# Two buffers and one sum of the last group, its reload's sequence, and the written unit order of a gated recurrent attention kernel

## The chip, the cores and the metric

The kernel runs on one core of one Trainium2 chip. A core has five engines that each work through a list of instructions in order: TensorE (PE, matrix multiplies), VectorE (DVE), ScalarE (ACT), GpSimd (POOL) and SyncE (SP, which here only issues DMAs). They wait for each other by semaphores. The metric is the time of one execution in microseconds of device time, the median of several.

## The reference

Two branches work on the same `x` (2048 rows of 512) and are mixed row by row by a gate.

```python
g = _sigmoid((x * gate_w).sum(-1, keepdims=True))
a = _A_ref(x, A_mem0, A_Wq, A_Wk, A_Wv, A_Wo, A_seg_len)
b = _B_ref(x, B_wq, B_wk, B_wv, B_wo, B_beta)
return g * a + (1 - g) * b
```

Branch A is a recurrence over 64 segments of 32 rows. Each segment takes the 8 memory rows that the segment before it left, puts its 32 rows behind them, and runs attention with 32 heads of 128 over these 40 rows:

```python
for s in range(n_seg):
    h = jnp.concatenate([mem, xs], axis=1)
    q, k, v = (jnp.einsum('btd,dhe->bhte', h, W) for W in (Wq, Wk, Wv))
    scores = jnp.where(mask[None, None], jnp.einsum('bhqe,bhke->bhqk', q, k) * scale, -1e9)
    o = jnp.einsum('bhqk,bhke->bhqe', _softmax(scores), v)
    o = jnp.einsum('bhte,hed->btd', o, Wo)
    mem = o[:, :M, :].copy()
    outs.append(o[:, M:, :])
```

So segment s+1 can't begin before segment s has its output's first 8 rows. Branch B is a linear-attention layer over 4 blocks of 512 rows with 32 heads of 16; it depends on nothing in branch A.

## The kernel before, in words

**The work.** Everything is built as a list of operations for each engine. A planner class (`Prog`) derives the waits from what each operation reads and writes; an operation that overwrites a buffer waits for the buffer's readers, DMAs included. The order on each engine is the order in which the operations are recorded, and from segment 0 on that is the order of the names in one long string, `A_ORDER`, of 4,509 units. Before it stand the loads, the projections of branch B and the gate (up to some 50.8 us in the profile).

**Names in the order.** `s.Kbx` and `s.Kby` are the two halves of the projection of keys for half b (16 heads) of segment s on PE (line 1272; 8 matmuls each), and so for Q and V; Q1 is split otherwise (line 1498). Small letters (`s.k0`, `s.v1`) are the evacuations from PSUM, `T..` the transposes on DVE, `Z` a bias matmul, `S` scores (lines 1558 and 1563), `X` the exponential, `Y` the mask (1576), `M` the row sums on PE (1591), `L` logarithm and exponential on ACT that make the reciprocal (1598, 1601), `N` and `n` the multiplications by it on DVE (1605) and POOL (1610). `s.PV` is the product with the values, called pv (1622) and pvL (1633) on PE; `E0` to `E3` evacuate it into `OT_sb`; `W0` to `W3` are the four output passes on PE, called wo (1359; 1371 in the last segment). `s.hm` turns the first 8 rows into the next segment's memory on DVE (1659 to 1664), `s.H` evacuates all rows to `WN` and `s.ws` stores them to DRAM (`aTd`). A `~` behind a name swaps ACT and DVE for that unit's evacuation.

**Left rows.** A segment has 40 rows, 8 more than a multiple of 32. The last 8 of each of the 4 segments of a group g are done together: `Lg.xl` gathers them (line 1297), `Lg.KL..`, `QL..` and `VL..` project them, and the values go to DRAM and back in another layout: a store when both halves are evacuated (line 1305) and the reload `Lg.VLt` (line 1313), which pvL of the group's segments reads. `Og.0` to `Og.3` are their output passes (ol on PE, line 1359), `Og.e` evacuates them to `WN` (olev), `Og.s` stores them to `aTl` (sto).

**The tail of a group.** `Tg.l` reloads 128 rows of both stores into `AR` (one DMA per segment and store, lines 1422 and 1424), `Tg.a` adds the two halves of `AR` on POOL (asum, 1428), `Tg.b` is branch B's output product on PE (brow, 1441; for the last group also browz, 1451), `Tg.t` scales it by 1 - g into AR's first half (t1, 1459; t1z, 1464), `Tg.f` multiplies, adds and stores the result (fin, 1471; out, 1473). Group 15 is the last; its fourth segment, 63, has its own short way: finz (1668) and four small stores (1672).

**Branch B.** `pj` and `pp` are late projections of the last block and their evacuations (lp on PE, line 830), `bS` scores (926), `bE` exponentials (947) and masks, `bP` the product with the values (979), `bT` what follows. `wl` loads one of eight pieces of Wo (line 540). The last bP is in segment 58; from there on the buffers `KTj` (keys) and `PT` (probabilities) of branch B are not used any more.

Of the kernel before, what the change touches and what calls it, by code (L numbers as in the profile page):

```python
# [1769 lines left out]
```

## Time and profile before

| what | us |
| --- | --- |
| median of 3 executions | 839.45 (837.83 to 843.68) |
| the profiled execution | 840.33 |
| its span, first to last instruction | 838.3 |
| PE busy in the span | 791.7 |
| DVE, ACT, POOL busy | 582.7, 566.0, 290.0 |
| mean granted clock of TensorE | 0.991 |

The profile is of one execution. "L1272" is line 1272 of the kernel before. "Busy" is the time in which an engine has an instruction under way; PE's matmuls are pipelined, so their ends overlap the next one's start. A bracket at the end of a timeline row holds the idle time of the engine before the row and what ended it. "SPq" rows are DMAs as SP issues them; they land later. The granted clock of TensorE is a share of its full speed.

### The profile page before, as it was taken

What the parts mean: (1) busy time and instruction counts of PE and PEld (TensorE: products, weight loads), DVE (VectorE), ACT (ScalarE), POOL (GpSimd) and SP (SyncE); (2) the same over time, 40 slices, a digit from 0 to 9 for tenths busy, and PEclk for the clock granted to TensorE, in tenths of its full rate; (3) what the DMA queues carried; (4) which work ended last, traced back from release to release, by engine and by line L of the source; (5) the groups of instructions that cost most, each with busy time, mean ns of one, the idle gap of its engine ahead of it and who ended that gap; (6) DMA issues with size and microseconds to landing.
All of it is one profiled execution on the core that took longest, in us unless ns stands there. A gap on an engine that the chain in (4) does not pass through costs nothing.

```text
span 838.3 us, 51677 instructions
## 1 busy us (share of the span) xinstructions
PE 791.7 (94%) x23285; PEld 487.1 (58%) x23291; DVE 582.7 (70%) x1469; ACT 566.0 (68%) x1368; POOL 290.0 (35%) x728
## 2 busy tenths in 40 slices
PE   8997999999999999999999999999999999999885
PEld 4544566555575656556556556566656556556553
DVE  4556677767677677787767686687676778687553
ACT  5544777877768667777657877685676775886452
POOL 4501443432424343342522434252233332453121
PEclk9998999999999999999999999999999999999998
DMA  8995332122222122112213031122122122121221
GB/s 330 415 373 180 88 93 73 39 65 71 52 63 81 38 63 62 46 45 78 64 30 94 28 78 46 42 51 70 54 71 72 35 57 66 39 52 41 74 79 52
DMA packets 100632, 72.34 MB, mean 86 GB/s; under 512 B 58068, under 2 KB 94524, under 8 KB 98876
## 3 DMA queue, kind: packets, MB, share of 16 engines
q1 hardware_dynamic: 99692, 68.24, 26.6%
q8 instruction: 182, 2.98, 1.5%
q10 hardware_dynamic: 720, 0.80, 0.3%
q14 instruction: 38, 0.31, 0.1%
HBM read 43.43 MB, written 25.58 MB: 82 GB/s over the span
## 4 chain that ended last, share of the span: by engine, by line
PE 74%; DVE 8%; ACT 7%; DMA 5%; issue 3%; POOL 2%; SPq 1%; ACTq 0%; DVEq 0%; POOLq 0%
PE ps L1272 35%; PE ps L1359 15%; PE ps L1498 6%; PE ps L1622 3%; PE ps L926 2%; PE ps L979 2%; DMA scr_kqd<-stgk 2%; ACT PT L947 2%; POOL PT L953 2%; PE ps L1558 1%; PE ps L692 1%; PE ps L1591 1%; PE ps L1441 1%; ACT R_sb L1601 1%; DVE oTt L1003 1%
## 5 line engine op out<-in xcount | busy, mean ns | idle before, releaser
L947 ACT ACTIVATE PT<-ps 128x512 bf16<-128x512 f32 x320 | 171.9, 603 | 55.2 <-PE ps L926 47.2
L953 POOL TENSOR_SCALAR_AFFINE_SELECT PT<-PT 128x128 bf16<-128x128 bf16 (+2 forms) x320 | 121.5, 380 | 213.5 <-ACT PT L947 195.1
L1272 PE MATMUL ps<-Wv_sb,xTp 128*32 128x512 bf16 x2048 | 144.0, 379 | 0.0
L1272 PE MATMUL ps<-Wk_sb,xTp 128*32 128x512 bf16 x2048 | 132.8, 379 | 1.8 <-DVE xTp L1664 1.5
L1359 PE MATMUL ps<-Wo_sb,OT_sb 128*32 128x256 bf16 x4032 | 125.2, 275 | 7.7 <-ACT OT_sb L377 3.6
L1359 PEld LDWEIGHTS ps<-Wo_sb,OT_sb 128*32 128x32 bf16 x4032 | 103.4, 97 | 29.5 <-ACT OT_sb L377 22.2
L1610 POOL TENSOR_TENSOR P_sb<-P_sb,R_sb 128x64 bf16<-128x64 bf16 x128 | 49.9, 390 | 160.9 <-ACT R_sb L1601 155.1
L377 ACT ACTIVATE OT_sb<-ps 128x320 bf16<-128x320 f32 x174 | 65.2, 439 | 36.5 <-PE ps L1633 35.8
L1272 PEld LDWEIGHTS ps<-Wk_sb,xTp 128*32 128x32 bf16 x2048 | 56.1, 97 | 52.1 <-DVE xTp L1664 7.8
L377 ACT ACTIVATE KN_sb<-ps 128x512 bf16<-128x512 f32 x98 | 58.8, 603 | 40.0 <-PE ps L1272 38.9
L377 ACT ACTIVATE QN_sb<-ps 128x256 bf16<-128x256 f32 (+1 forms) x148 | 64.6, 438 | 26.8 <-PE ps L1272 24.8
L1498 PE MATMUL ps<-Wq_sb,xTp 128*32 128x256 bf16 x2048 | 71.6, 273 | 2.4 <-DVE xTp L1664 2.0
L1284 DVE STREAM_TRANSPOSE QT_sb<-QN_sb 128x128 f32<-128x128 f32 (+1 forms) x192 | 63.2, 335 | 12.8 <-ACT QN_sb L377 10.5
L1272 PE MATMUL ps<-Wq_sb,xTp 128*32 128x512 bf16 x1024 | 70.2, 381 | 1.4 <-DVE xTp L1664 0.8
L1572 ACT ACTIVATE P_sb<-ps 128x224 bf16<-128x224 f32 x128 | 45.6, 358 | 34.1 <-PE ps L1563 28.6
L1284 DVE STREAM_TRANSPOSE KT_sb<-KN_sb 128x256 f32<-128x256 f32 x128 | 55.8, 437 | 18.4 <-ACT KN_sb L377 15.2
L379 DVE CAST V_sb<-ps 128x512 bf16<-128x512 f32 x80 | 54.8, 687 | 18.9 <-PE ps L1272 17.0
L1498 PEld LDWEIGHTS ps<-Wq_sb,xTp 128*32 128x32 bf16 x2048 | 54.6, 97 | 20.6 <-DVE xTp L1664 7.3
L1659 DVE STREAM_TRANSPOSE tt<-ps 128x256 f32<-128x256 f32 x63 | 28.3, 450 | 50.8 <-PE ps L1359 50.3
L379 DVE CAST OT_sb<-ps 128x320 bf16<-128x320 f32 x82 | 37.5, 486 | 28.6 <-PE ps L1633 27.7
L1605 DVE TENSOR_TENSOR P_sb<-P_sb,R_sb 128x160 bf16<-128x160 bf16 x128 | 42.3, 340 | 16.5 <-ACT R_sb L1601 15.7
L1272 PEld LDWEIGHTS ps<-Wv_sb,xTp 128*32 128x32 bf16 x2048 | 44.8, 95 | 12.9 <-ACT QN_sb L377 1.0
(143 smaller groups left out, 1413.7 us busy)
## 6 DMA issues: line engine op xcount, KB each, us to landing
scr_aTd<-WN SPq DMA_DIRECT2D x63, 128.0 KB, 2.1
AR<-scr_aTd SPq DMA_DIRECT2D x63, 96.0 KB
Wk_sb<-in_A_Wk_dram SPq DMA_DIRECT2D x4, 1024.0 KB, 11.1
Wq_sb<-in_A_Wq_dram SPq DMA_DIRECT2D x4, 1024.0 KB, 14.5
Wv_sb<-in_A_Wv_dram SPq DMA_DIRECT2D x4, 1024.0 KB, 13.8
Wo_sb<-in_A_Wo_dram SPq DMA_DIRECT2D x8, 512.0 KB, 7.4
scr_vld<-VNL SPq DMA_DIRECT2D x16, 256.0 KB, 2.1
VL<-scr_vld SPq DMA_DIRECT2D x64, 64.0 KB
```

Of the source, the lines that this page charges most:

```text
L377: P.op("act", lambda a: a.activation(dst, src, ACT.Copy), reads=[v.rbank[k] for k in bks], writes=dres, name=name)
L379: P.op("dve", lambda d: d.tensor_copy(dst, src), reads=[v.rbank[k] for k in bks], writes=dres, name=name)
L947: P.op("act", lambda a: a.activation(pt, v.pb[bk], ACT.Exp, scale=v.SCALE_B), reads=[v.rbank[bk]], writes=[rp], name="be%d_%d" % (n, t))
L953: P.op("gp", lambda g: g.affine_select(mv, mv, [[0, len(cut)], [1, 128]], ALU.is_ge, 0.0, base=0, channel_multiplier=-1), reads=[rp], writ ...
L1272: ins = pe.matmul(pb[bk][SEG * j:SEG * (j + 1), :], lhs(c), cols(w, j) if split else w[:, 512 * j:512 * (j + 1)], start=(c == 0), stop=(c ...
L1284: P.op("dve", lambda d: d.transpose(to, src), reads=reads, writes=writes, name=name)
L1359: ins = pe.matmul(pb[bk][SEG * j:SEG * (j + 1), 0:256], lhs(h), Wo_sb[:, h, :].rearrange("p (k q c) -> p q k c", q=2, c=64)[:, j % 2], sta ...
L1498: ins = pe.matmul(pb[bk][SEG * j:SEG * (j + 1), 0:256], lhs(c), cols(w_sb[:, c, 2048 * b + 1024 * half:2048 * b + 1024 * (half + 1)], j), ...
L1572: P.op("act", lambda a: a.activation(P_sb[:, b, :], pb[bk][:, 0:So], ACT.Exp, scale=SCALE), reads=[rbank[bk]], writes=[Rs("Pm%d" % b), Rs( ...
L1605: P.op("dve", lambda d: d.tensor_tensor(wide[b][:, :, 0:L], wide[b][:, :, 0:L], R_sb[:, b, :].rearrange("p (i q) -> p i q", q=L), ALU.mult ...
L1610: P.op(ENG["n"], lambda d: d.tensor_tensor(left, left, grp04(R_sb[:, b, :]), ALU.mult), reads=[Rs("R0_%d" % b)], writes=[Rs("PL%d" % b)], ...
L1659: P.op("dve", lambda d: d.transpose(v.tt[:, :, :].rearrange("p (k n) t -> p k n t", n=2), src), reads=[rbank[wb["bk"]]], writes=[Rs("tt")] ...
```

## The change

It has four parts, all but the order for the last group (15) alone.

1. Its left rows are evacuated to `WZ`, which lies in `KTj`, instead of `WN`.
2. Its scaled rows (t1) go to `t1y`, which lies in `PT`, instead of the first half of `AR`; the sum of AR's halves is done by DVE instead of POOL.
3. Its reload issues first the three DMAs from `aTd` and then the three from `aTl`, instead of by turns.
4. `A_ORDER` is another sequence of the same units. It differs in segments 0 to 7 (but for 3), around 9 and 10, 13 to 22, 45 to 47 and 52 to 63; the rest is the same. Its first and its last lines are shown.

```diff
+    v.WZ = v.KTj[0][:, :].bitcast(F32)
+    v.t1y = v.PT[0][:, :, :].rearrange("p a w -> p (a w)").bitcast(F32)
...
 A_ORDER = """
-    0.Q0x~ wl L0.xl 0.Q1x 0.Q0y~ bS~ L0.KL1x 0.q0 L0.KL0x 0.K1x bE L0.KL1y pj bE 0.K1y 0.Q1y~ L0.KL1e~ pj 0.TQ0 0.k1 L0.KL0y~ wl L0.VL0x L0.VL0y L0.VL1x
-    0.q1x bE wl L0.VL1y L0.VL0e 0.K0x L0.QL1x 0.q1y 0.Z1 wl 0.TQ1x pj L0.VL1e~ L0.QL0x wl 0.K0y pp~ 0.V0x~ 0.V0y~ L0.QL0y~ L0.QL1y 0.v0~ L1.xl wl 0.k0~
-    L0.KL0e L1.KL0x L0.QL1e~ wl 0.TK0 0.V1x~ pj 0.TK1 L0.QL0e~ L1.QL0x 0.qt bE 0.TQ1y L1.KL1x 0.S1 0.S0 L1.KL1y 0.V1y 0.X1 0.X0 0.Y0 L1.KL1e~ 0.M1 L1.KL0y
-    L1.QL0y 0.M0 L1.QL1x L1.QL1y L0.VLt pj 0.L1 wl pp~ 0.v1 bP 1.qt 0.N1 0.L0 0.N0 bP 0.n0 pj 0.n1 L1.QL1e~ 0.PV 0.E0 0.E3 0.E1 0.W0 0.E2~ 0.W1 0.W2
-    L1.KL0e~ pp 0.W3 bS~ 1.Z1 0.hm bE 0.H~ 1.Q0x L1.QL0e~ bE 1.Q0y~ 1.K0x 1.K0y~ bE 1.Q1x 1.K1x 1.q0 bE 1.k0 1.K1y~ 1.TQ0 1.TK0 1.S0 1.Q1y~ bP 1.q1x
+    L0.xl pj L0.KL1x 0.Q1x~ pj bS bE 0.q1x bE 0.K1x~ L0.KL1y~ 0.K1y wl bE L0.QL1x L0.KL1e~ L0.QL1y L0.VL1x 0.k1 L0.VL0x 0.TK1 L0.VL0y L0.VL1y 0.K0x~ bE
+    L0.QL1e 0.Q0x L0.QL0x 0.V1x~ 0.V1y~ L0.KL0x wl 0.TQ1x pp~ 0.Q0y~ L0.VL0e~ L0.KL0y~ 0.V0x~ 0.Q1y L0.QL0y L0.VL1e~ wl 0.q1y 0.v1 0.K0y pj wl 0.V0y
+    L0.KL0e L1.xl 0.q0~ L1.QL0x 0.k0 L1.QL1x L1.KL1x 0.TQ1y 0.TK0 0.TQ0 L0.QL0e~ L1.KL0x L1.KL1y~ 0.qt 0.Z1 0.S0~ 0.S1~ wl 0.X0 pj 0.X1 0.Y0 L1.KL0y~ 0.M1
+    L1.QL0y wl 0.L1 0.M0 pj L0.VLt wl L1.QL1y~ 0.L0 0.n0 L1.KL1e 0.N1 0.n1 bP 0.v0 0.N0 L1.QL1e~ wl L1.KL0e~ 0.PV~ pj bP pp 0.E0 0.W0 0.E3 0.E2~ 0.E1~ bS
+    bE 0.W1 bE bE 0.W2 0.W3 0.hm bE bP pp 1.qt 1.Z1 L1.QL0e~ 0.H bP 1.K0x~ 1.Q0x~ 1.K0y~ 1.Q0y~ 1.k0~ 1.TK0 1.q0~ 1.K1x 1.K1y 1.k1 1.Q1x 0.oL 1.Q1y 1.q1x
...
-    62.k1 62.Q1x~ 62.TK0 61.ws 62.TK1 62.q1x 62.Q1y 62.qt 62.q1y 62.S0 62.X0 62.TQ1x 62.TQ1y 62.V0x 62.V1x 62.S1 62.X1 62.Y0 62.M0 62.V1y~ 62.v1 62.L0
-    62.M1 62.L1 61.oL 62.V0y 62.n0 62.v0~ 62.n1 62.N0 62.N1 62.PV~ 62.E0 62.W0 T14.l 62.E1~ 62.E3~ 62.E2~ 62.W1 62.oL 62.W2 62.W3 O15.0 62.hm 63.qt O15.1
-    O15.2 63.Q1y O15.3 T14.a 63.K0x~ 62.H 62.ws T14.b O15.e 63.K1x~ 63.Q1x 63.q1y 63.K1y T14.t O15.s 63.k1 T14.f 63.Q0x T15.l 63.Q0y 63.q0 63.TK1 63.q1x
-    63.TQ1y 63.V1x 63.V0x 63.K0y 63.TQ1x 63.S1 63.V0y 63.TQ0 63.k0~ T15.b 63.TK0 63.v0 63.V1y 63.S0 63.X1 63.M1 63.X0 63.Y0 63.M0 63.L0 63.v1 63.L1 63.n0
-    63.N0 63.N1 63.n1 63.PV 63.E0 T15.a 63.W0 63.E1~ 63.W1 63.E2 63.E3 T15.t 63.W2 63.W3 63.H T15.f
+    62.K1x T13.f 61.oL 62.K1y~ 62.TQ0 62.k0 62.k1 62.TK0 62.Q1y T14.l 62.q1y~ 62.S0 62.Q1x 62.TK1 62.V0x 62.X0 62.q1x 62.Y0 62.TQ1y 62.M0 62.V0y~ 62.TQ1x
+    62.L0 62.S1~ 62.X1 62.n0 62.V1x~ 62.M1 61.H 62.V1y 62.v0 62.N0 62.L1 62.v1~ 62.n1 61.ws 62.N1 T14.b 62.PV 63.Z1 62.E0 62.E3~ 62.E1 62.W0 62.E2 62.oL
+    62.W1 62.W2 62.W3 63.qt O15.0 O15.1 62.hm O15.2 O15.3 T14.a 62.H 63.K0x~ O15.e~ 62.ws T14.t 63.Q0x 63.K0y~ O15.s 63.Q0y~ 63.Q1y 63.K1x~ T14.f 63.q0~
+    63.k0~ 63.TK0 63.K1y~ 63.q1y 63.k1 63.TQ0 63.Q1x 63.TQ1y 63.q1x~ 63.TK1 T15.l 63.S0~ 63.V0x~ 63.V1x~ 63.X0 63.TQ1x 63.V0y~ 63.S1 63.Y0 63.M0 63.X1
+    63.v0 63.V1y 63.M1 63.L0 63.L1 63.n0 63.v1 63.N0 63.n1 63.N1 T15.b 63.PV T15.t 63.E0 63.E2~ 63.E3 63.E1~ 63.W0 63.W1 63.W2 63.W3 T15.a 63.H T15.f
 """
...
+        late = g == ngrp - 1
+        WL, rl = (v.WZ, Rs("jK0")) if late else (v.WN[:, :], Rs("WN"))
...
-            evac(ENG["O0"], v.WN[:, :], pb[st["bk"]][:, 0:256], [st["bk"]], [Rs("WN")], "olev%d" % g)
+            assert not late or bat.pv_n == bat.total
+            evac(ENG["O0"], WL, pb[st["bk"]][:, 0:256], [st["bk"]], [rl], "olev%d" % g)
...
-            rows_out(v.aTl[g], v.WN[:, :], [Rs("WN")], Rs("aTl%d" % g), P.group("sl%d" % g, "sl"), "sto%d" % g)
+            rows_out(v.aTl[g], WL, [rl], Rs("aTl%d" % g), P.group("sl%d" % g, "sl"), "sto%d" % g)
...
+        t1, rt = (v.t1y, [Rs("PT0"), Rs("PT1")]) if last else (t1_sb[:, :], [Rs("t1_")])
...
-            for r in range(3 if last else 4):
-                P.dma(grp, lambda sp, r=r: sp.dma_start(rows[SEG * r:SEG * (r + 1) - M], v.aTd[4 * g + r].rearrange("(k t) w -> t k w", k=4)[M:SEG]),
...
+            order = [(r, b) for b in range(2) for r in range(3)] if last else [(r, b) for r in range(4) for b in range(2)]
+            for r, b in order:
+                if b:
...
-            P.op("gp", lambda gq: gq.tensor_tensor(aTg[0:top, :, :].rearrange("p c t -> p (c t)").rearrange("p (k q c) -> p q k c", q=2, c=64),
+            P.op("dve" if last else "gp", lambda gq: gq.tensor_tensor(aTg[0:top, :, :].rearrange("p c t -> p (c t)").rearrange("p (k q c) -> p q k c", q=2, c=64),
...
-            P.op("act", lambda a: a.activation(t1_sb[:, :], pb[bb], ACT.Copy, scale=omg_sb[:, g:g + 1]),
-                 reads=[rbank[bb], Rs("omg")], writes=[Rs("t1_")], name="t1_%d" % g)
+            assert not last or bat.pv_n == bat.total
+            P.op("act", lambda a: a.activation(t1, pb[bb], ACT.Copy, scale=omg_sb[:, g:g + 1]),
+                 reads=[rbank[bb], Rs("omg")], writes=rt, name="t1_%d" % g)
...
-            P.op("dve", lambda dv: dv.scalar_tensor_tensor(fin[0:top], fin[0:top], g_sb[0:top, g:g + 1], t1_sb[0:top, :], ALU.mult, ALU.add),
-                 reads=[Rs("g"), Rs("t1_")], writes=[Rs("aTg")], name="fin%d" % g)
+            P.op("dve", lambda dv: dv.scalar_tensor_tensor(fin[0:top], fin[0:top], g_sb[0:top, g:g + 1], t1[0:top, :], ALU.mult, ALU.add),
+                 reads=[Rs("g")] + rt, writes=[Rs("aTg")], name="fin%d" % g)
```

More of the change, by code (lines that the diff above doesn't have):

```diff
@@ L1075 @@
[L1075 to L1076 removed]
+    bE pj 4.K0x 4.K0y bE bE 4.Q0x bT 3.H~ 3.ws 4.Q0y~ 4.K1x~ 4.k0 4.K1y 4.q0~ L1.VLt bP pp bT 4.TK0 4.k1 4.Q1y bP 4.TQ0 L2.xl 4.Q1x~ 4.S0~ bS 4.q1y~
+    4.V1x~ 4.TK1 4.TQ1y 4.q1x~ 4.X0 4.TQ1x 4.V1y 4.Y0 bE 4.v1 4.Z1 bE 4.S1~ bE 4.V0x~ 4.M0 4.X1 4.V0y~ 4.L0 4.M1 4.n0 pj pj 4.v0 4.L1 4.n1 bE 4.N0 pj 4.N1
@@ new lines @@
+    38.N0 L10.QL0x 38.v1~ 38.N1 bT bP 39.qt 38.PV 38.E0 L10.QL0y 38.E1~ 38.E3 37.ws 39.Z1 38.E2 38.W0 38.W1 38.W2 38.W3 L10.QL0e 38.hm bS L10.VL0x bE
+    L10.VL0y 39.Q0x bE L10.VL0e 39.K0x 39.Q0y 39.K0y~ bE 39.K1x~ 39.K1y~ 39.Q1y bE 39.q0~ 39.k0 39.Q1x 39.k1 39.q1y 39.TQ0 39.TK0 39.TK1 39.S0~ 38.oL
+    39.V0x 39.TQ1y 39.q1x 39.V0y~ 39.X0 39.TQ1x 39.S1~ 39.Y0 39.M0 39.X1 bP 38.H~ 39.V1x 39.M1 39.V1y 38.ws 39.v0 L10.QL1x 39.L0 39.N0 39.L1 39.n0
+    L10.VL1x 39.n1 39.N1 39.v1~ 39.PV 39.E0 39.E2~ L10.VL1y 39.E1~ bP 39.E3~ 39.W0 39.W1 39.W2 39.W3 bT L10.QL1y L10.VL1e~ 39.hm bS~ bT L10.QL1e~ 40.Q1x~
```

332 lines of the change are left out of this document (164 added, 168 removed).

## The prediction

> **What bounds the kernel now.** I read the page's head, then the table of windows by stage, then windows, timeline, waits and chain of the two worst stages.
>
> ```profile
> span 838.3 us, 51677 instructions
> PE 791.7 (94%) x23285; PEld 487.1 (58%) x23291; DVE 582.7 (70%) x1469; ACT 566.0 (68%) x1368; POOL 290.0 (35%) x728
> ```
> ```profile
> 50.80:79.30 28.50, 23.74 (x525) 12.51 (x528) 14.83 (x36) 10.95 (x24) 3.37 (x11) 0.89 0.86 280
> 79.30:160.00 80.70, 78.11 (x2340) 47.19 (x2344) 59.41 (x146) 59.61 (x141) 31.75 (x85) 1.00 0.29 76
> 160.00:776.00 616.00, 595.39 (x18469) 370.48 (x18464) 453.60 (x1159) 440.82 (x1083) 221.12 (x514) 1.00 0.21 56
> 776.00:815.70 39.70, 34.73 (x1144) 21.98 (x1140) 22.13 (x59) 20.62 (x55) 9.23 (x19) 1.00 0.29 80
> 815.70:838.30 22.60, 13.62 (x456) 9.05 (x444) 8.50 (x20) 6.24 (x17) 3.20 (x4) 0.83 0.17 49
> ```
>
> A window row gives the stretch, its length, the busy time of PE, PEld, DVE, ACT and POOL, PE's granted clock, DMA share and GB/s. PE is the bound, and the change takes no matmul off it, so it can win only PE's idle time and time at a lowered clock. The middle (79.3 to 776) has 80.7 - 78.1 + 616.0 - 595.4 = 23.2 us idle in 697, or 3.3%. Segment 0 (50.8 to 79.3) has 4.8 idle in 28.5 and a clock of 0.89; segments 59 to 62 have 5.0 in 39.7; the last 22.6 us have 9.0 and a clock of 0.83. So the two ends decide. There I cut stretches of 3.41 us at the points where the clock changes:
>
> ```profile
> 69.44:72.85 3.41, 1.40 (x52) 0.64 (x48) 1.66 (x5) 0.39 (x1) 0.31 (x1) 1.00 0.99 257
> 72.86:76.27 3.41, 2.26 (x48) 1.63 (x52) 2.01 (x5) 1.55 (x3) 0.00 (x0) 0.50 0.30 99
> 76.27:79.68 3.41, 2.92 (x52) 1.35 (x48) 1.60 (x6) 1.17 (x3) 0.31 (x2) 0.50 0.12 41
> 810.13:813.54 3.41, 2.11 (x104) 1.01 (x96) 1.83 (x5) 2.22 (x7) 0.76 (x2) 1.00 0.55 161
> 827.20:830.62 3.42, 1.19 (x92) 1.08 (x96) 1.37 (x4) 2.38 (x8) 2.13 (x3) 1.00 0.02 5
> 830.62:834.03 3.41, 2.55 (x92) 2.03 (x80) 0.29 (x2) 0.77 (x2) 0.00 (x0) 0.50 0.00 0
> ```
>
> The clock is halved right after the stretches in which PE was busy 1.40 and 1.19 us, not after the one with 2.11: the limit lies between 1.40 and 2.11 of 3.41. The second loss (830.62) hits the last matmuls.
>
> **The change, part by part. Start (segment 0).**
>
> ```profile
> 73.47 0.30 PE L1633 MATMUL ps<-P_sb,VL 32*128 32x64 bf16 x8 [2.21 <-DMA VL<-scr_vld]
> 74.31 3.60 PE L1359 MATMUL ps<-Wo_sb,OT_sb 128*32 128x256 bf16 x64 [0.54 <-ACT OT_sb L377]
> 79.25 1.02 PE L1272 MATMUL ps<-Wq_sb,xTp 128*32 128x512 bf16 x12 [0.48 <-ACT PT L947]
> ```
> ```profile
> 56.28 3.08 SPq L540 DMA_DIRECT2D Wo_sb<-in_A_Wo_dram  x4
> 62.59 2.13 SPq L540 DMA_DIRECT2D Wo_sb<-in_A_Wo_dram  x2
> ```
> ```profile
> 59.89 7.25 DMA scr_vld<-VNL
> 69.06 4.28 DMA VL<-scr_vld
> 783.62 2.59 PE ps L1272 x48
> 779.43 1.96 PE ps L1359 x64
> ```
> ```profile
> Wo_sb<-in_A_Wo_dram SPq DMA_DIRECT2D x8, 512.0 KB, 7.4
> Wv_sb<-in_A_Wv_dram SPq DMA_DIRECT2D x2, 1024.0 KB, 10.2
> L530 SPq DMA_DIRECT2D Wv_sb<-in_A_Wv_dram x4: 423/458/1128, 27.5 to 45.1; - x4
> ```
>
> PE waits 2.21 us for the left values (VL, L1633), whose way is evacuation, store (L1305; 7.25 us to land, behind four Wo pieces of L540 issued before it), reload (L1313; 4.28 us). Then the four output passes of segment 0 (L1359) run at half clock: 3.60 us against 1.96 for the same 64 matmuls at 779.43. Segment 1 starts at 79.25.
>
> The new order first adds a wait. VL1x, the first pass that needs Wv, now stands behind nine passes of 0.43 us (2.59 / 6, six passes of 8 matmuls) and the bS (a pass's 0.43 at most; I take 0.33): 50.8 + 4.2 = 55.0. Wv's last piece, issued at 45.1, lands 9.5 to 10.9 later (10.9 is twice the median of the last two, 10.2, less the least, 9.5), by 56.0: PE waits 1.0, with all of its queue behind it. Up to pv0 (L1622) stand 37 passes, bS, a bias, two scores, two sums and a bP, together 17.1: PE is there at 50.8 + 17.1 + 1.0 = 68.9. DVE's order puts a value evacuation before the second multiplication that pv0 needs (0.74 is DVE's row of that size, fin15 below), so pv0 runs at about 69.7 (before: 73.47 - 2.21 - 0.4 = 70.9).
>
> On SP's queue the VL store now has two Wo pieces ahead of it instead of four, and Wo3 and Wo7 go behind the reload. So 1 MB less is ahead of the store; at the stage's 280 / 0.86 = 325 GB/s that is 3.2 us: it lands at about 64, not 67.1. The reload still queues behind the Wo pieces already issued, less Wo3 (1.6 us): it lands at 73.3 - 1.6 = 71.7. Ends: 70.9 (last issue at 66.6, plus its 4.28) and 73.3 (nothing gained). I take 72.0, as the bytes ahead are what made the row. Wo3 and Wo7, issued after the reload at some 67 to 68.5, land by their median of 7.4 at 75.9 or before, about when wo0_3 comes (76).
>
> Idle from 70.1 to 72.0, and 0.8 before pv0, still lets a stretch like 69.4 to 72.9 fall under the limit, so I keep the half clock, but for one stretch, since lp2_1 and bP1, moved behind pvL, make the next one full. From 72.0: pvL 0.3, lp2_1 0.43, bP 0.11, wo 1.96, bS 0.33 (bS now splits the output passes) = 3.1, plus 1.7 for 3.41 us at half clock: 76.8. The new states reach segment 1 1.14 us after the last wo (DVE L1659 at 781.42, first pass at 782.56, below): 77.9, and two bP of 0.12, paid later before, are done. Start: -1.35 - 0.25 = **-1.6**. Ends: -3.3 with the clock kept, +0.3 if VL lands at 73.3 and both stretches stay at half clock.
>
> **Middle.** About 30 of 64 segments are reordered. Laying the orders side by side, I counted PE work between the last sum and pv, between pvL and wo0, and behind wo3. Most are as before; segment 21 loses its ol pass behind pvL (+0.57, the wait of an uncovered wo0 below), 45 has 0.67 instead of 1.12 behind wo3 (+0.45); 46 has 0.66 instead of 0.22 behind pvL (-0.35), 22 and 52 gain before pv (-0.2). **+0.5**, ends -1 and +3 (the other queues could hide a new wait).
>
> **End (segments 59 to 63).**
>
> ```profile
> 781.42 0.46 DVE tt L1659
> 782.56 1.06 PE ps L1498 x32
> 816.58 3.60 DMA scr_aTd<-WN
> 820.48 0.38 ACT QN_sb L377
> 824.38 0.86 PE ps L1441 x16
> ```
> ```profile
> PE ps L1622 <- ACT V_sb L377: 1.8, 2, 0.9
> PE ps L1498 <- DVE xTp L1664: 1.0, 2, 0.7
> PE ps L1558 <- DVE QT_sb L1284: 0.5, 1, 0.5
> ```
> ```profile
> 826.88 0.28 PE L1591 MATMUL ps<-P_sb,onesb 128*32 128x160 bf16 x8 [0.72 <-DVE P_sb L1576]
> 828.86 0.37 PE L1622 MATMUL ps<-P_sb,V_sb 32*128 32x40 bf16 x32 [1.70 <-DVE P_sb L1605]
> 829.14 1.27 POOL L1428 TENSOR_TENSOR aTg<-AR 96x512 bf16<-96x512 f32 x1 [0.17 <-POOL P_sb L1610]
> 829.90 2.23 PE L1371 MATMUL ps<-Wo_sb,OT_sb 128*32 128x128 bf16 x98 [0.57 <-ACT OT_sb L377]
> 830.44 0.69 ACT L1459 ACTIVATE AR<-ps,omg_sb 128x512 f32<-128x512 f32 x1
> 832.67 1.04 PE L1371 MATMUL ps<-Wo_sb,OT_sb 128*32 128x128 bf16 x30 [0.53 <-issue]
> 834.01 0.74 DVE L1471 SCALAR_TENSOR_TENSOR aTg<-aTg,g_sb,AR 96x512 bf16<-96x512 bf16 x1
> ```
>
> - Left rows in KTj (WZ) instead of WN: olev15 waited 3.60 us on ACT until segment 62's store had read WN, with a Q evacuation, t1_14 and a K evacuation behind it; Q and K led to the 0.5 before the scores (L1558). Now it runs on DVE behind the states (0.4, off PE's path), and the wait goes: **-0.45**. Next late there are the K0/Q0 evacuations, with four passes (1.74) in front: covered, as in the middle's segments.
> - brow14 (0.86, L1441) moves from segment 63, where PE had other work, to just before pv62, one of the two 0.9 waits for V: **-0.85**. pv59's 0.9 stays.
> - ol15_3 moves ahead of segment 63's first pass, whose wait was 1.0 - 0.67: **-0.35**. In 59 to 61 one ol and one QL pass trade places behind pvL and wo3: 0.
> - Three value passes now stand between the two scores, so the 0.72 before sum63 (826.88) goes: **-0.7**.
> - brow15 and browz (0.86 and a quarter of it) move from before that sum to before pv63, into the 1.70 wait. The 1.70 held the reciprocals of both halves, one behind the other; now the first half's is done during the last value pass. One alone I put at 1.2 (ends 0.85, its half, and 1.70), so 1.2 stands where 1.1 + 1.70 stood: **-1.6**.
> - t1_15 writes PT, no longer AR's first half, which asum15 reads until 830.41 on POOL; it goes ahead of the OT evictions on ACT. With t1z it takes about 1 (0.69 and a row a quarter as wide) from the end of brow15 on and holds the first eviction back by 0.3, and wo63 with it: **+0.3** (ends 0 and +1).
> - asum15 goes from POOL to DVE, between the last OT eviction and finz: 0.74 if priced by fin15 (the DVE row of this size), beside 1.96 of wo63. Without that cover it is +0.74, at most 1.27.
> - The reload takes its three aTd pieces first, so they don't queue behind sto15's landing. Before, asum15 waited for POOL's own queue (the bracket at 829.14), not for the reload: 0. If the pieces came late, the wait would be DVE's, ahead of finz, and cost from the moment wo63 ends.
> - Clock: 829.90 to 833.71 is 3.81 for what takes 1.96 at full clock. With the waits filled no 3.41 us has more than about 1.2 idle: **-1.85**.
>
> Sum -5.5; ends -3.0 and -6.5. What follows wo63 (finz, fin15, stores: 4.6) stays.
>
> [...]
>
> **Sum.** -1.6 + 0.5 - 5.5 = -6.6 from the profiled execution's 840.33 us (span 838.3, 2.0 around it): 833.7. That execution lies 0.88 above the median of 839.45; I take half of this as its extra loss to the clock: 839.9 - 6.6 = **833.3**, own range 831 to 836.5.
>
> **Rivals.**
> 1. *Clock kept at the start.* VL lands by 71, or the stretches fall otherwise, and segment 0 runs at full clock: 1.7 more, 831.6. For: idle falls by about a microsecond. Against: 0.8 + 1.9 idle is still there.
> 2. *The half clock isn't these gaps'.* It stays at both ends, so 1.85 of the tail and 1.3 of the start are not won: 836.5. Against: both losses follow the two emptiest stretches.
> 3. *The new queue order brings the left values no sooner.* They land at 73.3 as before: start 0 instead of -1.6: 834.9. For: DMA is 0.99 busy there.
> 4. *Slower: new waits in the reordered middle.* Place: pvL to wo0, where the OT eviction costs 0.57 once nothing stands between. It decides at 6.1 / 0.57 = 11 segments; at 17 it gives 843. For: an order only counts on PE, while evictions and SP's queue moved too. Against: the count shows only 21 and 59 losing cover.
>
> **How the numbers follow.** Forecast 0.50, rivals 0.18, 0.12, 0.10, 0.10. About 1% (8.4 us) is what a measurement of this kernel tells from no change: below 831.05 lie nearly half of rival 1 and 0.14 of the forecast's 0.5, so faster 0.18; above 847.85 a part of rival 4, 0.04; same 0.78. The range, 829.5 to 840.5, goes from the low ends (start -3.3, middle -1) to past rivals 2 and 3 and leaves out rival 4 and a little below: under 0.2.
>
> **What would show it.** Windows after: clock 1.00 up to the last matmul, wo63 in about 2 us, and 50.8 to segment 1's first pass in about 27 us. Waits: none for WN's store, none near 1.70 before pv63, one of about 1 us at VL1x for Wv, about 1.9 at pvL for VL. It is wrong if the middle's idle leaves 22 to 26 us, or if VL's wait grows.

## The result, and the profile after

The changed kernel takes 835.03 us (median of 16 executions, 831.54 to 839.5), the kernel before on the same chip 840.38 (16 executions, 837.51 to 844.11). The ratio is 0.9936, with a 95% interval of 0.9918 to 0.9954: 5.4 us faster (3.9 to 6.9). The forecast was 833.3, with a range of 829.5 to 840.5. The profiled execution took 835.36, with a span of 833.4.

To see where the time went I cut both traces at the same units: the end of the last matmul ahead of the order, the states of segment 3, the states of segment 58, and the issue of the last output. The windows view, first of the kernel before, then of the changed kernel (columns as in the prediction):

```profile
50.85:118.68 67.83, 61.57 (x1650) 34.83 (x1652) 42.25 (x102) 39.03 (x91) 18.88 (x51) 0.95 0.54 163
118.68:771.33 652.65, 631.01 (x19548) 392.60 (x19540) 482.27 (x1230) 469.62 (x1151) 237.09 (x558) 1.00 0.21 57
771.33:836.35 65.02, 52.96 (x1704) 33.74 (x1704) 33.94 (x85) 29.60 (x79) 12.72 (x23) 0.96 0.25 73
```
```profile
50.32:116.20 65.88, 59.94 (x1648) 34.81 (x1652) 41.00 (x100) 39.65 (x93) 18.95 (x51) 0.97 0.57 173
116.20:770.53 654.33, 631.25 (x19548) 394.87 (x19540) 483.30 (x1231) 469.61 (x1149) 236.18 (x558) 1.00 0.21 57
770.53:831.49 60.96, 52.00 (x1704) 34.28 (x1704) 35.75 (x91) 28.59 (x74) 11.64 (x22) 0.99 0.27 77
```

The stretches hold the same PE work (1704 matmuls in both last rows; the few missing in the first are missing records). The start became 1.95 us shorter, the middle 1.68 longer, the end 4.06 shorter; before all of them the changed execution was 0.53 earlier. How much of this is the change, and how much the one execution, the experiments show.

Segment 0 in the changed kernel, its stretches of 3.41 us, the way of the left values from the chain of waits, and PE's timeline:

```profile
68.94:72.35 3.41, 0.38 (x32) 0.27 (x32) 1.71 (x5) 1.44 (x3) 0.30 (x1) 1.00 1.11 291
72.35:75.77 3.42, 3.16 (x52) 1.52 (x56) 0.89 (x2) 1.00 (x3) 0.00 (x0) 0.50 0.58 193
```
```profile
58.69 5.89 DMA scr_vld<-VNL
66.73 5.74 DMA VL<-scr_vld
```
```profile
53.19 0.62 PE L1274 MATMUL ps<-Wk_sb,xTp 128*32 128x512 bf16 x8 [0.70 <-ACT PT L949]
...
55.56 1.26 PE L1274 MATMUL ps<-Wv_sb,xL 128*32 128x512 bf16 x20
...
69.92 0.38 PE L1633 MATMUL ps<-P_sb,V_sb 32*128 32x40 bf16 x32 [1.14 <-ACT LN_sb L379]
72.61 0.30 PE L1644 MATMUL ps<-P_sb,VL 32*128 32x64 bf16 x8 [2.32 <-DMA VL<-scr_vld]
...
78.02 0.29 PE L981 MATMUL ps<-PT,Vj 128*32 128x256 bf16 x4 [0.96 <-POOL PT L955]
...
78.34 0.60 PE L1274 MATMUL ps<-Wk_sb,xTp 128*32 128x512 bf16 x8
```

The store (5.89) landed at 64.6, forecast about 64, and the reload (5.74) at 72.5, forecast 72.0. PE stood 1.14 before pv0 and 2.32 before pvL0; the stretch up to 72.35 has 0.38 busy, and one stretch at half clock follows it. PE did not wait for Wv. It waited 0.70 at 53.19 for a bank of PSUM that branch B's exponential had not read yet, and reached VL1x at 55.56, when Wv was there. A last wait (0.96, for a mask on POOL, L955) stands just ahead of segment 1, whose first pass comes at 78.34, where 77.9 was forecast. Counted from the first cut, that is 28.0 us, against 28.4 in the kernel before. The end, as the timeline has it, and a stretch of the windows view that holds the last matmul:

```profile
822.80 1.04 PE L1451 MATMUL ps<-woB_sb,oTg 128*32 128x512 bf16 x16
...
823.66 0.40 PE L1461 MATMUL ps<-woB_sb,oTg 128*32 128x128 bf16 x16
...
824.18 0.37 PE L1633 MATMUL ps<-P_sb,V_sb 32*128 32x40 bf16 x32
...
825.22 1.63 PE L1373 MATMUL ps<-Wo_sb,OT_sb 128*32 128x128 bf16 x102 [0.57 <-ACT OT_sb L379]
825.53 0.68 DVE L1438 TENSOR_TENSOR aTg<-AR 96x512 bf16<-96x512 f32 x1
828.27 0.57 PE L1373 MATMUL ps<-Wo_sb,OT_sb 128*32 128x128 bf16 x26 [1.42 <-issue]
828.88 0.35 DVE L1679 SCALAR_TENSOR_TENSOR KTL<-ps,g_sb,KTL 128x128 bf16<-128x128 f32 x1 [2.67 <-PE ps L1373]
```
```profile
826.70:830.11 3.41, 0.71 (x36) 0.39 (x25) 1.01 (x2) 0.00 (x0) 0.00 (x0) 1.00 0.00 0
```

brow15 (L1451) and browz (L1461) fill the place in front of pv63, asum15 (L1438) runs on DVE beside wo63 (L1373), and the clock stays at 1.00 past the last matmul. But wo63 is split: after 102 of its matmuls PE stands for 1.42 us, with "issue" as the reason, so for nothing that the profile shows. From its first to its last matmul it takes 3.62 us, which is hardly less than the 3.80 that it took at half clock before. The waits view sums such times; first the kernel before, then the changed one:

```profile
PE ps L1359 <- issue: 3.4, 5, 1.2
PE ps L1371 <- issue: 0.5, 1, 0.5
```
```profile
PE ps L1361 <- issue: 4.2, 6, 1.3
PE ps L1373 <- issue: 1.4, 1, 1.4
PE ps L1274 <- issue: 1.0, 3, 0.5
```

All rows of PE with "issue" that the view lists add up to 5.0 us in the kernel before and to 7.8 in the changed one.

### The profile page after: what moved, and what is told of

The parts are those of the page before. It is cut to its first block, busy times and chain, and to the rows that moved or that the text cites. A ratio compares the mean times of both kernels' runs of the same rounds, so it can differ in the third digit from the quotient of the medians.

```text
span 833.4 us, 51666 instructions
## 1 busy us (share of the span) xinstructions
PE 789.1 (95%) x23285; PEld 489.9 (59%) x23291; DVE 584.3 (70%) x1475; ACT 565.6 (68%) x1363; POOL 288.0 (35%) x727
## 3 DMA queue, kind: packets, MB, share of 16 engines
q8 instruction: 182, 2.98, 1.6%
## 4 chain that ended last, share of the span: by engine, by line
PE 77%; DVE 8%; ACT 6%; DMA 4%; issue 3%; POOL 2%; SPq 1%; ACTq 0%; DVEq 0%; POOLq 0%
PE ps L1274 37%; PE ps L1361 16%; PE ps L1509 6%; PE ps L1633 3%; PE ps L928 2%; PE ps L981 2%; ACT PT L949 2%; DMA scr_kqd<-stgk 2%; PE ps L1569 2%; PE ps L1602 2%; PE ps L694 1%; POOL PT L955 1%; PE ps L1451 1%; DVE oTt L1005 1%; PE ps L832 1%
## 5 line engine op out<-in xcount | busy, mean ns | idle before, releaser
L955 POOL TENSOR_SCALAR_AFFINE_SELECT PT<-PT 128x128 bf16<-128x128 bf16 (+2 forms) x320 | 120.3, 376 | 214.4 <-ACT PT L949 197.4
L379 ACT ACTIVATE QN_sb<-ps 128x256 bf16<-128x256 f32 (+1 forms) x153 | 67.0, 442 | 34.2 <-PE ps L1274 29.0
L379 ACT ACTIVATE OT_sb<-ps 128x320 bf16<-128x320 f32 x169 | 63.3, 439 | 34.4 <-PE ps L1644 33.8
L379 ACT ACTIVATE KN_sb<-ps 128x512 bf16<-128x512 f32 x97 | 58.1, 602 | 40.8 <-PE ps L1274 40.2
L381 DVE CAST OT_sb<-ps 128x320 bf16<-128x320 f32 x87 | 39.4, 485 | 26.6 <-PE ps L1644 26.3
```

The costliest lines, as they stand in the source:

```text
L379: P.op("act", lambda a: a.activation(dst, src, ACT.Copy), reads=[v.rbank[k] for k in bks], writes=dres, name=name)
L381: P.op("dve", lambda d: d.tensor_copy(dst, src), reads=[v.rbank[k] for k in bks], writes=dres, name=name)
L955: P.op("gp", lambda g: g.affine_select(mv, mv, [[0, len(cut)], [1, 128]], ALU.is_ge, 0.0, base=0, channel_multiplier=-1), reads=[rp], writ ...
```

## The experiments

The theory after the result: the two ends gained as forecast through filled waits and a kept clock, and wo63 lost 1.4 us because PE waited for its own instructions. Its rivals: the half clock has another cause; the issue stall hangs on the moment or on data; the parts of the order do not add up. Line numbers of the experiments differ from those of the changed kernel by up to 4, or by 8 behind an inserted filler. Every number in microseconds against the kernel before is the ratio of the two times, applied to 840.

**The order in three parts.** Positions in the order at which both orders have issued the same units allow a switch from one to the other.

```
x1_tail:  changed kernel; units 1 to 4222 in the old order, the rest in the new
x2_start: kernel before;  units 1 to 360 in the new order, the rest in the old
x3_mid:   kernel before;  units 361 to 4222 in the new order, the rest in the old
```

> The changed kernel with the old order up to the start of segment 59 and the new order behind it (parts 1 to 3 as changed). The forecast's theory: the end alone is worth -5.5 us, so about 834.9 against 840.4 of the kernel before, with no wait over 1 us before pv63 and full clock up to the last matmul. Second theory, read off the trace of the changed kernel (segment 63 won 4.0 us and segments 59 to 62 nothing, as a stall of 1.4 us inside wo63 took a part back): -4.0, so 836.4, with such a stall in wo63 again. Rival: the end's gain hangs on what the new order does further ahead; then it is under -2.

> The kernel before with only the first 360 units of the order new (segments 0 to 3); all else old. The forecast's theory: -1.6 us, 838.8, with one half-clock stretch of 3.41 us in place of 6.83. The marks of the changed kernel's trace: -2.0 to -2.5 at the end of segment 3, of which 0.5 was there before the first changed unit, so -1.5 to -2.5 if later segments keep it. Rival: segments behind it give it back (PE work only moved from one segment to the next), 0 to -0.8.

> The kernel before with only the units 361 to 4222 of the order new (segments 4 to 58). The forecast's theory: +0.5 us, 840.9. The marks of the changed kernel's trace: between segment 3 and segment 58 the lead fell from 2.5 to 0.8 us, so +1.7, 842.1. Rival of the forecast (new waits in the middle): +3 or more.

Measured: x1_tail 0.9972 (0.9949 to 0.9996), -2.4; x2_start 0.9982 (0.9955 to 1.001), -1.5; x3_mid 1.0006 (0.9984 to 1.0029), +0.5. The signs are those of the forecast, and the sum, -3.4, agrees with -5.4 within the intervals of some 2 us each, which also means that the times alone separate little. The interval of x1_tail (-0.3 to -4.3) leaves out the -5.5 of the forecast for the end and takes in the -4.0 of the second theory, whose stall came again: wo63 takes 3.04 us there. The traces say more. The three windows in every profiled execution of this study, cut at the same units:

| kernel | start | middle | end | order in the three |
| --- | --- | --- | --- | --- |
| before | 67.8 | 652.7 | 65.0 | old, old, old |
| x4_fill | 65.7 | 653.1 | 63.4 | old, old, old (end with filler) |
| x1_tail | 68.2 | 650.7 | 59.8 | old, old, new |
| x2_start | 67.8 | 652.3 | 64.1 | new, old, old |
| x3_mid | 66.2 | 652.7 | 64.1 | old, new, old |
| after | 65.9 | 654.3 | 61.0 | new, new, new |
| x5_wo64 | 67.8 | 653.2 | 59.1 | new, new, new |
| x6_fillpv | 69.0 | 652.5 | 60.2 | new, new, new (start with filler) |
| x7_warm | 66.2 | 657.2 | 60.4 | new, new, new |
| x8_left | 67.0 | 654.4 | 60.4 | new, new, new |
| x10_left2 | 67.9 | 655.5 | 62.8 | new, new, new |
| x12_brow | 64.5 | 654.3 | 61.9 | new, new, new |
| x9_wide | 65.1 | 653.6 | 59.8 | new, new, new (start with filler) |
| x11_both | 66.7 | 650.0 | 58.1 | new, new, new (start with filler) |

The end falls apart cleanly: 64.1 to 65.0 with the old order (without filler), 59.8 to 61.0 with the new one where nothing in it is altered (x1_tail, after, x7_warm). At the start the same order gives 65.7 to 68.2 (old) and 64.5 to 67.9 (new, without filler): the 1.95 us between the two profiles shown is mostly chance, and the means differ by 0.3 (67.0 and 66.7). The middle varies by several us for one and the same order, so the 1.68 there is no measure of the order either.

**The half clock.** In x4_fill the kernel before gets nothing but work for PE in the 1.70 us before pv63.

```diff
+                v.fill = lambda: P.op("pe", f_, reads=[Rs("oTg"), Rs("woB")], writes=[rbank[bb]], name="fill")
...
             bks = held[0] = B.four()
+            if last:
+                v.fill()
+                v.fill()
```

> The kernel before, and nothing new but brow15's 16 matmuls issued twice more (1.7 us of PE work whose result is the same) just before pv63, in the 1.70 us in which PE waits there. The forecast's theory: the half clock behind comes of that gap, so filling it keeps the clock at 1.00 and wo63 takes 1.96 instead of 3.81: -1.85 at most, about -1.4 if some of it goes to PE's own issue stalls. Rival (the half clock is not due to this gap): clock halved at the same place, 0.

Measured: 0.9994 (0.9972 to 1.0016), -0.5, so the times do not tell the two apart. The profile does. PE's timeline and two stretches, one at the end and one at the start:

```profile
825.33 1.90 PE L1441 MATMUL ps<-woB_sb,oTg 128*32 128x512 bf16 x32
827.21 0.37 PE L1626 MATMUL ps<-P_sb,V_sb 32*128 32x40 bf16 x32
...
828.25 1.97 PE L1371 MATMUL ps<-Wo_sb,OT_sb 128*32 128x128 bf16 x128 [0.57 <-ACT OT_sb L377]
```
```profile
71.74:75.15 3.41, 1.60 (x56) 1.19 (x56) 1.82 (x5) 0.93 (x2) 0.00 (x0) 1.00 0.65 207
826.08:829.49 3.41, 2.84 (x152) 1.93 (x146) 1.14 (x3) 2.41 (x8) 2.13 (x3) 1.00 0.02 5
```

The stretch before wo63 is 2.84 busy, the clock stays at 1.00, and wo63 takes 1.97 in place of 3.81. The rival falls: the half clock was the gap's. The mean granted clock, which is on record for every execution, says the same: 0.9976 over the 12 of x4_fill, 0.9941 over the 35 of the kernel before beside them. The row at 71.74 shows what nobody had changed: in this execution the old start kept its clock. Its wait for the left values was 1.51 us there, and the stretch had 1.60 busy. In x8_left (below) a stretch with 1.58 was still followed by half clock:

```profile
70.26:73.67 3.41, 1.58 (x52) 0.83 (x44) 1.33 (x4) 0.89 (x3) 0.00 (x0) 1.00 1.05 307
```

Yet busy time alone does not decide. Of two more stretches with the same 1.79, the one in x10_left2 (first two rows; PE's waits there were 1.14 and 0.86) was followed by half clock, and the one in x5_wo64 (last two rows) was not:

```profile
69.42:72.84 3.42, 1.79 (x72) 1.07 (x76) 2.13 (x5) 1.99 (x5) 0.14 (x1) 1.00 0.97 309
72.84:76.25 3.41, 3.41 (x66) 2.03 (x68) 0.17 (x1) 2.58 (x5) 1.54 (x5) 0.50 0.09 28
68.74:72.15 3.41, 1.79 (x67) 0.84 (x58) 2.84 (x8) 2.68 (x7) 0.63 (x2) 1.00 0.98 242
72.15:75.56 3.41, 2.12 (x63) 1.28 (x67) 0.89 (x2) 1.10 (x3) 0.00 (x0) 1.00 0.82 256
```

How a wait lies in the stretches changes from one execution to the next, and with it the loss: of four profiles with the old start one had two stretches at half clock (the profile shown before), two had one and one had none; of seven with the new start and no filler five had one and two none. x6_fillpv and x9_wide fill the changed kernel's wait before pvL0, the first with four more pv0 (128 small matmuls), the second with 21 wide ones.

```diff
+            if s == 0:
+                for n in range(4):
+                    P.op("pe", f_main, reads=[Rs("VN0"), Rs("VN1"), Rs("Pm0"), Rs("Pm1")], writes=[rbank[k] for k in bks], name="fill%d" % n)
...
+                    for n in range(21):
+                        ins = pe.matmul(pb[bks[0]][:, 8 * L:512], v.warm[:, 0:128], v.warm[:, 0:512 - 8 * L], start=False, stop=False, skip_group_check=True)
```

> The changed kernel with segment 0's pv0 issued four times more (4 x 0.37 = 1.5 us of PE work whose result is the same) in the wait between pv0 and pvL0. The theory that the half clock comes of PE's idle time in a 3.41 us stretch: no half clock at 72 us, -1.7 against the changed kernel (833.3), less up to 0.4 if the left values land before the filler is done. Rival: the start's half clock has another cause; it stays, 0. The 256 more instructions are just one packet, so by the theory of the instruction queue wo63 stalls at the same place, about 1.4.

> The changed kernel with a filler in segment 0 between pv0 and pvL0: 21 matmuls of 192 columns of zeros into unused columns of a bank (about 1.7 us of PE work in 42 instructions; the filler before, 128 small matmuls, was itself held up 1.1 us for instructions and left the stretch at 1.20 of 3.41 busy). From ten profiles so far: half clock follows stretches with PE busy 0.38 to 1.59 of 3.41, and not those with 1.60 or more. So with the filler no stretch at 69 to 73 is under 1.6, the clock is 1.00 up to the last matmul, and segment 0 is 1.7 us shorter than with one half-clock stretch: -1.7 against the changed kernel, 833.3. Rival: the executions differ so much in where the grid falls that the mean gain is a part of that, -0.5 to -1.

```profile
70.46 0.69 PE L1633 MATMUL ps<-P_sb,V_sb 32*128 32x40 bf16 x68 [1.14 <-ACT LN_sb L379]
72.22 0.92 PE L1633 MATMUL ps<-P_sb,V_sb 32*128 32x40 bf16 x92 [1.07 <-issue]
```
```profile
68.94:72.35 3.41, 1.19 (x99) 0.73 (x91) 2.04 (x5) 1.70 (x4) 0.69 (x2) 1.00 1.14 304
```
```profile
829.07 0.57 PE L1373 MATMUL ps<-Wo_sb,OT_sb 128*32 128x128 bf16 x26 [0.63 <-issue]
```
```profile
71.19 1.91 PE L1643 MATMUL ps<-aTg 128*128 128x192 bf16 x21
```

Measured: x6_fillpv 0.9955 (0.9929 to 0.9981), no better than the changed kernel: after 36 of the filler's matmuls PE stood 1.07 us for "issue", the stretch stayed at 1.19 busy, and the clock was halved. wo63 stalled at the same place as in the changed kernel, behind 102 matmuls, for 0.63 where 1.4 was expected (the row at 829.07). x9_wide 0.9921 (0.9896 to 0.9946): its filler ran through, and the clock was 1.00 up to the last matmul; over its ten executions the mean granted clock is 0.9991, over the changed kernel's 16 it is 0.9970. Against the changed kernel that is -1.3, with intervals too wide to tell -1.7 from the rival's -0.5 to -1.

**The stall in wo63.** x5_wo64 does it in half the instructions and leaves out the sum of the two halves; x7_warm moves every later instruction by 42 places.

```diff
-            (out_whole if last else out_part)(wb["bk"], k, first, lambda h: OT_sb[:, h, q], [Rs("OT%d" % k)], "wo%d_%d" % (s, k))
+            out_part(wb["bk"], k, first, lambda h: OT_sb[:, h, q], [Rs("OT%d" % k)], "wo%d_%d" % (s, k))
...
-        for n in range(WARM):
-            ins = pe.matmul(v.pb[bk], v.warm[:, 0:128], v.warm[:, :], start=True, stop=True)
+        for n in range(4 * WARM):
+            ins = pe.matmul(v.pb[bk][:, 0:128], v.warm[:, 0:128], v.warm[:, 0:128], start=True, stop=True)
```

> The changed kernel with the last segment's output done as in the other segments: 64 matmuls of 256 columns for 128 of 128, the same columns in half the instructions; the two halves are not added, so the last 32 rows lack a part of their sum. Theory: the 1.4 us stall in the changed kernel's wo63 is PE waiting for its own instructions (the last 16-KB packet of the instruction queue starts at 825.96 and wo63, with 256 instructions in about 2 us, runs into its end). With half the instructions it does not get there: no stall, wo63 in 1.96 us, -1.4 against the changed kernel, so about 833.6. Rival: the stall hangs on the moment or on data (a DMA, the Wo buffer): it stays, 0.

> The changed kernel with its 7 warm-up matmuls of 512 columns, ahead of everything, done as 28 of 128: the same columns, 42 PE instructions more, so each later instruction lies 42 further on in the 256 of a packet. Theory of the instruction queue: the stall in wo63 comes 42 instructions earlier in wo63 (at its 160th of 256, not its 203rd), is of a similar size, and the other issue stalls move or go; total within 1 us of the changed kernel. Rival (stalls hang on the work, not on where packets end): the same places as in the changed kernel.

wo63 in x5_wo64, then in x7_warm:

```profile
826.85 1.93 PE L1361 MATMUL ps<-Wo_sb,OT_sb 128*32 128x256 bf16 x64 [0.57 <-ACT OT_sb L379]
```
```profile
827.97 1.35 PE L1373 MATMUL ps<-Wo_sb,OT_sb 128*32 128x128 bf16 x81 [0.57 <-ACT OT_sb L379]
830.18 0.85 PE L1373 MATMUL ps<-Wo_sb,OT_sb 128*32 128x128 bf16 x47 [0.86 <-issue]
```

With half the instructions there is no stall: 1.93. With 42 instructions ahead the stall (0.86) comes after 81 of the 128 matmuls, where it came after 102: 21 pairs of weight load and matmul, which are the 42 instructions. The times do not show it: 0.9938 (0.9915 to 0.9960) and 0.9940 (0.9918 to 0.9963). Of x5_wo64 -1.4 was expected, which intervals of some 2 us can't tell from nothing. I numbered every recorded PE instruction (weight loads, matmuls, semaphore instructions) in all fourteen traces: of 111 gaps over 0.5 us inside output passes 95 come right behind one number modulo 256, which is 186 in six of the traces and 192 in the eight that were taken later. The page of the profile has the queue that belongs to it:

```profile
q8 instruction: 182, 2.98, 1.6%
```

182 packets in 2.98 MB are 16,384 bytes each. For 256 instructions that is 64 bytes an instruction, and the 46,832 recorded PE instructions of the changed kernel are 182.9 times 256. x11_both (below), with 47,034, has 183 packets. The last stall of the changed kernel ends at 828.27, and the record of its packet starts at 825.96. In all 95 cases the packet that started last before PE went on is the one with the number of the block of 256 instructions that PE was about to enter, and PE goes on 2.19 to 3.10 us after its start. None of the 2,548 such borders in the fourteen traces is passed sooner than 2.17 us after its packet's start. So I read these gaps as PE standing where one packet of instructions ends and the next has not come.

By this reading the traces also say when a border can become a stall. The record of a packet started when PE was near the border before it (in 95 of 100 cases from 19 instructions ahead of it to 149 behind), and at full clock wo63 goes through 256 instructions in 1.97 us (x11_both, below). In x5_wo64 the last border lies 52 instructions ahead of wo63, and the 128 instructions of wo63 end before the next. So that run does not show that wider matmuls keep up: the output passes of the other segments have 256 columns and lose 4.2 us to "issue" in the changed kernel.

x11_both puts x9_wide's filler and 77 more small warm-up matmuls together, so that the last border falls on the beginning of wo63.

```diff
-        for n in range(WARM):
-            ins = pe.matmul(v.pb[bk], v.warm[:, 0:128], v.warm[:, :], start=True, stop=True)
+        for n in range(12 * WARM):
+            ins = pe.matmul(v.pb[bk][0:32, 0:64], v.warm[:, 0:32], v.warm[:, 0:64], start=True, stop=True)
```

> As the run with 21 filler matmuls, and the 7 warm-up matmuls done as 84 of 64 columns: together 196 more PE instructions, so the last packet's border, 52 instructions before the end of wo63 in the changed kernel, falls 248 before the end, at wo63's beginning, where PE waits 0.57 us anyway. Theory: no stall inside wo63 (2.0 us in place of 3.6), at most 0.5 at its beginning; other borders fall elsewhere too, with a total like before. -1.7 from the clock and -1 from wo63: about 832.4. Rival: the other borders cost more and it is no faster than the run without them.

```profile
820.61 1.97 PE L1373 MATMUL ps<-Wo_sb,OT_sb 128*32 128x128 bf16 x128 [0.57 <-ACT OT_sb L379]
```
```profile
PE ps L1361 <- issue: 1.5, 2, 1.0
PE ps L928 <- issue: 2.5, 3, 1.2
```

Measured: 829.65 us (6 executions, 828.47 to 832.14), ratio 0.9861 (0.9820 to 0.9901), -11.7: faster than both kernels, and by more than I expected. wo63 ran in 1.97. In the same series it is 4.7 us faster than x9_wide (829.65 against 834.35), and nothing but the warm-up lies between the two: 77 more matmuls, with 154 instructions, of a smaller shape. Most of the difference came in the middle, which is 3.6 us shorter (650.0 against 653.6). The output passes lost 1.5 us to "issue" in place of 4.6, but other lines lost more. All rows with "issue" together are 6.2 against 7.6, so stalls of this kind show for 1.4 of the 3.6, and the remainder is not explained. The same two rows of x9_wide and its wo63:

```profile
PE ps L1361 <- issue: 4.6, 6, 1.4
PE ps L928 <- issue: 1.8, 4, 0.6
```
```profile
824.25 1.99 PE L1373 MATMUL ps<-Wo_sb,OT_sb 128*32 128x128 bf16 x128 [0.57 <-ACT OT_sb L379]
```

There wo63 ran through too, with its border where x7_warm stalled. A border is no stall by itself: in x9_wide the packet started at 822.71, 2.68 us before PE passed the border, and in x7_warm at 827.85, 2.33 us before PE went on. Where a packet starts varies (the 19 instructions ahead to 149 behind of above), so I can't say from the order alone which borders become a stall.

**Two terms of the end.** x8_left and x10_left2 send the last left rows to WN again. In x8_left their evacuation overwrote what segment 62's store should read, so the wait that I was after was not in it; x10_left2 (first two places of the diff; x8_left has the first alone) has the store first. x12_brow (the last two) moves brow15 back.

```diff
-        late = g == ngrp - 1
+        late = False
...
-    62.W1 62.W2 62.W3 63.qt O15.0 O15.1 62.hm O15.2 O15.3 T14.a 62.H 63.K0x~ O15.e~ 62.ws T14.t
+    62.W1 62.W2 62.W3 63.qt O15.0 O15.1 62.hm O15.2 O15.3 T14.a 62.H 63.K0x~ 62.ws O15.e~ T14.t
...
-    63.TK1 T15.l 63.S0~
+    63.TK1 T15.l T15.b 63.S0~
...
-    63.N1 T15.b 63.PV
+    63.N1 63.PV
```

> The changed kernel with part 1 undone: group 15's left rows go to WN again. The forecast priced part 1 at 0.45 us. But in the new order their evacuation is on DVE behind the states, where it would wait for segment 62's store (3.6 us to land): I expect DVE to stand some 2 to 3 us there, with the K and Q evacuations of segment 63 behind it, +1 to +2.5 against the changed kernel. Rival: the order alone covers it, 0 to +0.45.

> The changed kernel with part 1 undone once more, now with segment 62's store issued ahead of the left rows' evacuation (before, the evacuation came first and overwrote what the store should read, so there was no wait to be seen). The evacuation, on DVE, now waits for that store (3.6 us to land). The forecast priced the wait at 0.45; I expect DVE to stand 2 to 3 us with K and Q evacuations behind it: +1 to +2.5 against the changed kernel. Rival: PE has enough other passes, 0 to +0.45.

> The changed kernel with brow15 and browz moved back ahead of segment 63's first scores, all else new. The forecast's theory: PE then waits 1.1 to 1.2 us before pv63 (its term for one half's reciprocal), so +1.1; the stretch around it keeps about 1.7 to 2.0 of 3.41 busy, so the clock stays in most executions, and where it falls under 1.6 it is +2 to +3. Rival: PE's other work covers it and nothing changes, 0.

DVE and PE in x10_left2, then PE in x12_brow:

```profile
823.03 0.42 DVE L381 COPY WN<-ps 128x256 f32<-128x256 f32 x1 [3.32 <-DMA scr_aTd<-WN]
...
823.51 1.05 PE L1272 MATMUL ps<-Wk_sb,xTp 128*32 128x512 bf16 x16 [1.15 <-DVE WN L381]
...
825.57 0.28 PE L1567 MATMUL ps<-QT_sb,KT_sb 128*32 128x40 bf16 x16 [0.58 <-DVE QT_sb L1284]
```
```profile
824.36 0.37 PE L1631 MATMUL ps<-P_sb,V_sb 32*128 32x40 bf16 x32 [1.20 <-DVE P_sb L1614]
```

x8_left (0.9945, 0.9921 to 0.9969) is as fast as the changed kernel and says nothing of the wait. In x10_left2 DVE stands 3.32 us for the store, and PE 1.15 and 0.58 behind it; the end is 1.8 longer than in the changed kernel (62.8 against 61.0). The times don't confirm the +1 to +2.5 that was expected: 0.9930 (0.9903 to 0.9957) is no slower than the changed kernel. So what part 1 is worth in time stays open between nothing and 1.8 us. x12_brow waits 1.20 before pv63 and keeps its clock (1.00 from 820.60 to 827.43): 0.9954 (0.9930 to 0.9979), 1.5 slower than the changed kernel where 1.1 was expected; the interval takes in the rival's 0 as well, but the wait in the trace is the one that was forecast.

## Why the prediction was right, and where it was not

The time lies in the range and 1.7 us above the forecast; of the -6.6 us the runs gave -5.4. The range alone says little, as it also takes in the 840.38 of the kernel before. Point by point:

- **PE is the bound, and only the two ends can win much.** Right for the end. For the start it holds in kind, but not in size (below).
- **End, -5.5.** The trace shows -4.06, and the difference of 1.4 is mainly one term. From the states of segment 58 to the start of pv63 the trace won 3.9 us, where the terms for the waits add up to 3.95. The waits went as forecast: none is left before sum63 or pv62, brow15 and browz stand where the 1.70 was, and the time of one half's reciprocal, taken as 1.2, is 1.20 in x12_brow. asum15 and the reload cost nothing. t1_15 cost nothing either (+0.3 forecast): 0.57 from pvL63 to wo63 as before.
- **The clock term, -1.85, is the step that was mis-sized.** Its mechanism is shown (x4_fill: 1.97 at full clock). But at full clock PE ran through wo63's 256 instructions faster than they came (1.97 us in x11_both; in no trace was a border passed sooner than 2.17 us after its packet's start), and stood 1.42 us in "issue": wo63 became 0.18 us shorter (3.62 against 3.80), not 1.85. In the other runs it takes 3.31 and 3.33 with the old order and half clock (x2_start, x3_mid), 2.8 to 3.6 at full clock with a stall, and 1.93 to 1.99 at full clock without one. The profile before had the sign of it: 0.53 us of "issue" in wo63 at half clock, in a row that I quoted and did not price.
- **Part 1, -0.45.** Too small for the trace: without it, in the new order, PE stands 1.7 us (x10_left2). By the times it stays open.
- **Start, -1.6.** Most events came within 0.5 us of the forecast (store, reload, pv0 at 69.9, one half-clock stretch), but the wait for Wv did not come, and a wait for a bank and one for a mask stood in its place. That pv0 still came near its forecast is luck. Up to segment 1's first pass the trace won 0.4 us of the 1.35 that the term has for it. VL's wait grew from 2.21 to 2.32, which the prediction names as a sign of being wrong: the values came 0.9 sooner (72.5 for 73.3), but PE reached pvL sooner still. Part of the mistake is the base: the profile before had two half-clock stretches, which three other executions of the same start did not have. Against an average execution little is left: the means of the traces differ by 0.3 (and x2_start's own start is as long as that of the kernel before, 67.8), x2_start says -1.5 with an interval from -3.8 to +0.8.
- **Middle, +0.5.** x3_mid says +0.5 (-1.3 to +2.4), the traces up to +2 with a spread of several us. The wait of an uncovered output pass, which the fourth rival needs in 11 more segments, did not become more frequent: 11 times and 4.2 us before, 9 times and 4.0 after. Waits for "issue" vary (4.2 us against 3.4 in the output passes), but that they make up the spread is not shown.
- **The limit for the half clock.** The prediction put it between 1.40 and 2.11 us of busy time. Its own rows have a stretch with 2.26 (at 72.86, itself at half clock) that was followed by another at half clock, so that limit does not hold behind a stretch at half clock.
- **Rivals.** The second (the half clock is not due to the gaps) is refuted at the end by x4_fill, and at the start by x9_wide, whose filler alone raised the mean granted clock to 0.9991. The first (the clock kept at the start) is no separate case: it happens in some executions (2 of 7). The third (left values no sooner) is wrong in its premise, since the store landed at 64.6 and not at 67.1. The reload took 5.74 in place of 4.28, though.

What stays open: how the -5.4 divides between start and middle, as intervals of 2 us and the spread of single executions cover it.

## What to carry to other kernels

Look for idle time near a clock that is lowered behind it, and price a filled gap by both (here 1.70 us of wait, and wo63 in 1.97 in place of 3.81 in x4_fill); but take such a loss from several profiles: in four profiles here the same old start had from none to two stretches at half clock. When a stretch of many small matmuls becomes faster, ask whether its instructions can keep up: "issue" rows in the waits were the sign (1.42 us in wo63). wo63 went without such a stall here with the border of a packet in another place (x11_both, 1.97), or in so few instructions that it ended before the border (x5_wo64, 1.93). Between two kernels, a part of the difference may be the place of those borders: x9_wide and x11_both have one order, and their "issue" rows differ by 1.4 us.

## What the runs showed of the hardware

- After the first 20 us of all fourteen profiles, a stretch of 3.41 us at full clock was followed by half clock when PE was busy at most 1.58 us of it, and not when it was busy 1.94 or more. In between, three stretches with 1.60 (x4_fill), 1.79 (x5_wo64) and 1.78 (x8_left) kept the clock, and one with 1.79 (x10_left2) did not. In that one PE's waits were 1.14 and 0.86 us.
- PE stood up to 1.6 us in an output pass for "issue" (x8_left), and 95 of 111 gaps over 0.5 us in output passes of the fourteen traces lie behind one number modulo 256 (186 in six of them, 192 in eight). The instruction queue of the changed kernel has 182 packets of 16,384 bytes for 46,832 PE instructions, 182.9 times 256. PE passed none of the 2,548 borders sooner than 2.17 us after the record of the next packet started. Waits for "issue" took 4.2 us in the output passes of the changed kernel and 1.42 in wo63.
- 77 more and smaller matmuls of warm-up, with 154 instructions, at the very start came with 829.65 us against 834.35 (x11_both, x9_wide); the two traces show 1.4 us of it as waits for "issue" (7.6 against 6.2).
